# Top-k attention and a gated feed-forward on one core: the steps behind the top-k are put in other slots and on other engines

## The chip, the core and the metric

The kernel runs on one core of a Trainium2 chip. The engines are named as the profile names them: PE is TensorE (PEld its weight loads), DVE is VectorE, ACT is ScalarE, POOL is GpSimd, SP is SyncE, whose queue issues most DMA transfers. Each engine works through its own list of instructions in order, and waits at an instruction until what it needs is there. The metric is the device time of one execution in microseconds (us); the profile's span, from the first to the last instruction, is a little shorter.

## The reference

```python
def _attn_ref(q, k, v):                       # each (8, 8, 576, 64), float32
    top_k = 32
    scale = 1.0 / np.sqrt(D)
    scores = scale * np.matmul(q, k.transpose(0, 1, 3, 2))
    kth = np.partition(scores, -top_k, axis=-1)[..., -top_k:-top_k + 1]
    scores = np.where(scores >= kth, scores, -1000000000.0)
    scores = scores - np.max(scores, axis=-1, keepdims=True)
    attn = np.exp(scores)
    attn = attn / (np.sum(attn, axis=-1, keepdims=True) + 1e-09)
    return np.matmul(attn, v)

def _moe_ref(x, w_in, w_out):                 # x: (4608, 512), the attention's output
    h = x @ w_in                              # (4608, 2048)
    g = h * np.clip(h + 3.0, 0.0, 6.0) / 6.0
    return g @ w_out                          # (4608, 512)
```

Per row of 576 scores only the 32 largest count in the softmax. The weights arrive as 64-bit floats and are made 32-bit floats on the chip (`convert`).

## The kernel before

A *pair* is two heads of one batch. A *duo* is one tile of 128 query rows of two pairs; the 64 rows left over of 576 make a *rest duo*, in which one tile holds both heads of a pair. There are 80 duos (64 full, 16 rest). The loop has eight *slots* a duo; in each, VectorE does one round of top-k (the eight largest by MAX8, then MATCH_REPLACE8 to strike them out), slots 0 to 3 for the first pair, 4 to 7 for the second:

```python
def top(self, u, r):
    ...
    for t in range(self.nt):                  # nt: 2 tiles, 1 in a rest duo
        nc.vector.max(self.m[u][:, t, 8 * r : 8 * r + 8], self.cur[t])
    if r < TOP_K // 8 - 1:
        for t in range(self.nt):
            nc.vector.match_replace(wk, self.m[u][:, t, 8 * r : 8 * r + 8], self.cur[t], LOWEST)
            ...
```

What follows the top-k of pair `u` goes through three engines and a transfer:

```python
def shift(self, u):                           # (32nd largest - largest) * scale
    nc.gpsimd.tensor_tensor(d[:, 0:nt], m[:, 0:nt, TOP_K - 1], m[:, 0:nt, 0], ALU.subtract)
    nc.gpsimd.tensor_scalar_mul(d[:, 0:nt], d[:, 0:nt], scale)
def exp(self, u):
    for t in range(nt):
        nc.scalar.activation(row, row, AF.Prelu, bias=m[:, t, TOP_K - 1 : TOP_K], scale=-1.0, alpha=FLAT)
    for t in range(nt):
        nc.scalar.activation(row, row, AF.Exp, bias=self.less[u][:, t : t + 1],
                             scale=-scale / FLAT, accum_out=self.den[:, u, t : t + 1])
    nc.scalar.activation(d, d, AF.Copy, bias=EPS)
def inverse(self, u):
    nc.vector.reciprocal(d, d)                # d = self.den[:, u, 0 : self.nt]
def weights(self, u):                         # rows times 1/den, then split in 16-bit halves
    nc.gpsimd.tensor_scalar(row, row, self.den[:, u, t : t + 1], 1.0, ALU.mult, ALU.mult)   # per t
    nc.gpsimd.tensor_copy(halves[:, :, to : to + c1 - c0], words)
def flip(self, u):                            # transpose by DMA
    nc.sync.dma_start_transpose(t16[:, 0:n, :], self.e16[u][:, 0 : n * P])
def join(self, u):                            # halves put together: eT
    copy = nc.gpsimd.tensor_copy if u and not self.early else nc.scalar.copy
```

`values` multiplies `eT` with v on TensorE into `pv`, `place` copies `pv` into `xT`, and every second duo gives a block of 128 tokens to `feed_forward`, which works in pieces of 8 matmuls of `h` or 2 of `acc`, sixteen to a block, about one to a slot:

```python
def feed_forward(xT, rows):
    for f0 in range(0, NFC, nf):              # 4 times 16 matmuls into h
        h = ps_w.tile([P, 512], F32, tag="w", name="h")      # one of 3 PSUM buffers
        ...                                   # a yield in the middle
        nc.scalar.activation(g[:], h[:], AF.Relu, bias=three[:], scale=1.0)
        nc.scalar.copy(hs[:], h[:])
        def gate(g=g, hs=hs):
            nc.gpsimd.tensor_scalar(g[:], g[:], 6.0, 0.0, ALU.min, ALU.max)
            nc.gpsimd.tensor_tensor(g[:], g[:], hs[:], ALU.mult)
        yield gate                            # emitted two pieces later
    ...                                       # 16 matmuls into acc, a yield after every second
```

`scores` puts q k^T into `big`, five PSUM banks (the only buffer of its kind), and ScalarE at once copies them into `sc`. Which part stands in which slot (counted from the duo's first; slot 8 is slot 0 of the next duo) is a table. Parts of one slot are emitted in the table's order, duo by duo, but all `shift` parts first:

```python
usual = dict(
    shift0=3, exp0=4, inverse0=9, weights0=10, flip0=12, join0=15,
    shift1=7, exp1=8, inverse1=13, weights1=14, flip1=16, join1=19, values=22, place=23,
)
behind = dict(usual, values=25, place=26)
early = dict(...)                             # duos 0 and 1
soon = dict(
    shift0=3, exp0=3, inverse0=5, weights0=5, flip0=7, join0=10,
    shift1=7, exp1=7, inverse1=9, weights1=9, flip1=11, join1=14, values=16, place=17,
)                                             # the last two duos
```

Of the kernel before, what the change touches and what calls it, by code (L numbers as in the profile page):

```python
# [29 lines left out]
def kernel(  # L30
# [65 lines left out]
    def convert(dst, src):  # L96

        st = kqpool.tile([P, 2 * WC], U32, tag="kq", name="st")
        nc.sync.dma_start(st[:], src)
        yield
        words = st[:].rearrange("p (n two) -> p n two", two=2)
        lo, hi = words[:, :, 0], words[:, :, 1]
        a = gpool.tile([P, WC], F32, tag="g", name="a")
        y = gpool.tile([P, WC], F32, tag="g", name="y")
        nc.scalar.activation(a[:], hi.bitcast(F32), AF.Abs)
        nc.gpsimd.tensor_scalar(a[:], a[:], HI_MOST, HI_LEAST, ALU.min, ALU.max)

        nc.scalar.activation(y[:], lo, AF.Copy, bias=2.0, scale=2.0**-51)
        yield

        au, yu = a[:].bitcast(U32), y[:].bitcast(U32)
        nc.vector.tensor_scalar(au, au, 3, None, ALU.logical_shift_left)  # L117
        nc.vector.scalar_tensor_tensor(  # L118
            out=yu, in0=hi, scalar=0x80000000, in1=yu,
            op0=ALU.bitwise_and, op1=ALU.bitwise_or,  # L120
        )
        yield
        nc.gpsimd.tensor_tensor(
            dst.bitcast(I32), a[:].bitcast(I32), y[:].bitcast(I32), ALU.add
        )
# [13 lines left out]
    class Pair:  # L139
# [6 lines left out]
        def load(self):  # L146
            h0 = 2 * self.hp
            t = self.landed = kqpool.tile([P, 2 * J + 1, 2, D], F32, tag="kq", name="landed")
            for i, src in enumerate((k, q)):
                for hh in range(2):  # L150
                    nc.sync.dma_start(
                        t[:, i * J : (i + 1) * J, hh, :],
                        src[self.b, h0 + hh, 0:JP, :].rearrange("(p j) d -> p j d", j=J),
                    )
                nc.sync.dma_start(
# [15 lines left out]
        def transpose(self):  # L171
            kq = kqpool.tile([P, JP + S], F32, tag="kq", name="kq")
            self.kT, self.qT = kq[:, 0:JP], kq[:, JP : JP + S]
            ps = big()
            for j in range(2 * J + 1):
                rows = self.landed[:, j, :, :].rearrange("p h d -> p (h d)")
                nc.tensor.transpose(ps[:, j * P : (j + 1) * P], rows, ident[:])  # L177
            c0 = 2 * JP
# [6 lines left out]
    class Duo:  # L185
# [14 lines left out]
        def scores(self, us=(0, 1)):  # L200

            if us[0] == 0:
                self.sc = scpool.tile([P, 2, 2 * (S + R)], F32, tag="sc", name="sc")
                self.den = mpool.tile([P, 2, 2], F32, tag="den", name="den")
            sc, nu = self.sc[:, us[0] : us[-1] + 1, :], len(us)
            ps = big()
# [4 lines left out]
            if self.rest:  # L211
                for i, u in enumerate(us):
# [5 lines left out]
                nc.gpsimd.memset(sc[:, :, S : S + R], 0.0)  # L218
                nc.scalar.copy(sc[:, :, 0:JP], banks[:, 0:nu, :])
                nc.scalar.copy(  # L220
                    sc[:, :, JP:S], left[:, 0 : nu * R].rearrange("p (u r) -> p u r", r=R)
                )
# [6 lines left out]
            for i, u in enumerate(us):  # L229
                pr = self.pairs[u]  # L230
                for hh, d in enumerate(heads):
                    nc.tensor.matmul(banks[:, 2 * i + hh, :], pr.qT[d, qs], pr.kT[d, :])  # L232
            nc.scalar.copy(  # L233
# [25 lines left out]
        def shift(self, u):  # L259

            nt, m = self.nt, self.m[u]
            d = self.less[u] = mpool.tile([P, 2], F32, tag="shift", name="shift")
            nc.gpsimd.tensor_tensor(
                d[:, 0:nt], m[:, 0:nt, TOP_K - 1], m[:, 0:nt, 0], ALU.subtract
            )
            nc.gpsimd.tensor_scalar_mul(d[:, 0:nt], d[:, 0:nt], scale)  # L266

        def exp(self, u):
# [7 lines left out]
            for t in range(nt):  # L276
                row = self.row(u, t)
                nc.scalar.activation(  # L278
                    row, row, AF.Exp, bias=self.less[u][:, t : t + 1], scale=-scale / FLAT,
                    accum_out=self.den[:, u, t : t + 1],  # L280
                )
            d = self.den[:, u, 0:nt]
            nc.scalar.activation(d, d, AF.Copy, bias=EPS)

        def inverse(self, u):
            d = self.den[:, u, 0 : self.nt]
            nc.vector.reciprocal(d, d)  # L287
# [64 lines left out]
    def feed_forward(xT, rows):  # L352
# [6 lines left out]
        for f0 in range(0, NFC, nf):  # L359
# [12 lines left out]
            g = gpool.tile([P, 512], F32, tag="g", name="g")  # L372
            nc.scalar.activation(g[:], h[:], AF.Relu, bias=three[:], scale=1.0)  # L373
            hs = hpool.tile([P, 512], F32, tag="h", name="hs")
            nc.scalar.copy(hs[:], h[:])
            gs.append(g)

            def gate(g=g, hs=hs):
                nc.gpsimd.tensor_scalar(g[:], g[:], 6.0, 0.0, ALU.min, ALU.max)  # L379
                nc.gpsimd.tensor_tensor(g[:], g[:], hs[:], ALU.mult)  # L380

            yield gate
        acc = ps_w.tile([P, DM], F32, tag="w", name="acc")
        for f in range(NFC):
# [7 lines left out]
            if f % 2 == 1:  # L392
                if f == NFC - 1:
                    o = opool.tile([P, DM], F32, tag="o", name="o")
                    nc.scalar.mul(o[:], acc[:], 1.0 / 6.0)  # L395
                    for p0, p1, dst in rows:
                        nc.sync.dma_start(dst, o[p0:p1, :])
                yield None

# [5 lines left out]
    for b in range(B):  # L405
        halves = [pairs[b][0:2], pairs[b][2:4]]
        for qt in range(J):
# [3 lines left out]
            if qt == (0 if b == B - 1 else J - 1) and not 2 < b < B - 1:  # L411
# [11 lines left out]
    gates = []  # L423

    def piece(count=1):
        nonlocal left
        for _ in range(count):
            while todo:
                try:
                    gates.append(next(todo[0]))  # L430
                    left -= 1
                    break
                except StopIteration:
                    todo.pop(0)
            else:
                gates.append(None)
            if len(gates) > 2:
                gate = gates.pop(0)
                if gate:
                    gate()  # L440
# [45 lines left out]
    def land(count=1):  # L486

        for _ in range(min(count, len(chunks))):
            c = convert(*chunks.pop(0))
# [20 lines left out]
    def pair_at(m, first):  # L510
# [5 lines left out]
    first[0].load()  # L516
    land(2)
    first[1].load()
    first[0].transpose()
    convert_step()  # L520
    duos[0].scores((0,))
    convert_step()
    first[2].load()
    convert_step()
    first[1].transpose()
    duos[0].scores((1,))
    land()


# [3 lines left out]
        shift0=3, exp0=4, inverse0=9, weights0=10, flip0=12, join0=15,  # L533
        shift1=7, exp1=8, inverse1=13, weights1=14, flip1=16, join1=19, values=22, place=23,
    )

    behind = dict(usual, values=25, place=26)
    early = dict(
        shift0=3, exp0=3, inverse0=4, weights0=4, flip0=5, join0=8,
        shift1=7, exp1=7, inverse1=8, weights1=8, flip1=9, join1=12, values=12, place=13,  # L540
    )
    soon = dict(
        shift0=3, exp0=3, inverse0=5, weights0=5, flip0=7, join0=10,
        shift1=7, exp1=7, inverse1=9, weights1=9, flip1=11, join1=14, values=16, place=17,
    )
    queued = {}
    for m in range(ND):
        for part, at in (early if m < 2 else soon if m >= ND - 2 else behind if per_batch <= m < ND - 4 else usual).items():
            queued.setdefault(8 * m + at, []).append((m, part))

    def parts(slot, late=None):

        for m, part in sorted(queued.get(slot, []), key=lambda x: x[1][:-1] != "shift"):
            if late is not None and (part[:-1] in ("inverse", "weights")) != late:
# [3 lines left out]
            elif part == "place":  # L558
                place(m)
            else:  # L560
# [3 lines left out]
    for m in range(ND + 3):  # L564
        u = duos[m] if m < ND else None
        for i in range(8):
# [7 lines left out]
            if m == 0 and i in (1, 2):  # L574
                first[i + 1].transpose()
            if i == (4 if m == 0 else 1) and m + 1 < ND:
                duos[m + 1].scores()
            if m < 4:
# [13 lines left out]
            if i == 5:  # L592
                p = pair_at(m, 5)
                if p:
                    p.transpose()

            due += ((left > 0) + (left >= 24) / 8 + (left >= 48) / 8) / (2 if u and u.rest else 1)
            piece(int(due))
            due -= int(due)
    while todo:  # L600
        piece()
    piece(2)
# [33 lines left out]
```

## Time and profile before

| | |
|---|---|
| device time, median of 3 runs | 1581.81 us (1580.72 to 1583.69) |
| span of the profile | 1578.5 us, mean granted TensorE clock 0.963 |
| MAX8, 1152 of them | 816.4 us busy |
| MATCH_REPLACE8, 864 | 635.5 us |
| reciprocals of `den`, 160 | 24.6 us |
| matmuls of the feed-forward (`h`, `acc`) | 1061.3 us |
| exponentials and PReLU on ScalarE, 576 | 430.5 us |
| shifts on GpSimd, 320 instructions | 69.4 us |

The rows are sums over groups of the same instruction. Busy times of neighbours overlap by some 0.07 us, so what an instruction costs its engine is better read from the distance between the starts of two. A row of idle time belongs to the engine that waits; it costs time only where that engine sets the end or holds up the one that does. Where a bracket follows a line of a timeline, it gives the idle time before it and what ended it.

### The profile page before, as it was taken

The numbers are of one execution on the slowest core, as the hardware profiler recorded it, in microseconds if no ns is written. First come the engines' busy times: TensorE is split into PE (matmuls) and PEld (weight loads), VectorE is DVE, ScalarE is ACT, GpSimd is POOL, SyncE is SP. The second block draws the span as 40 slices with busy tenths as digits, with TensorE's granted clock in tenths as the row PEclk, the third lists the DMA queues.
The fourth block names the chain that finished last, engine by engine and source line by source line (L and its number), as shares of the span: only waits on it lengthen the run. The fifth ranks groups of instructions, "written<-read, shape, count | busy, mean of one in ns | idle before, by whom it ended". The sixth has DMA issues, their size and how long they took to land.

```text
span 1578.5 us, 28787 instructions
## 1 busy us (share of the span) xinstructions
PE 1456.9 (92%) x10272; PEld 1039.0 (66%) x10272; DVE 1466.8 (93%) x3105; ACT 1096.3 (69%) x1865; POOL 1144.5 (73%) x1264
## 2 busy tenths in 40 slices
PE   5256799979999999998999999999999999999899
PEld 3153566567767777666777777776777767677675
DVE  6999999999999999999999999999999999999700
ACT  6675777777777777777776786777766787777621
POOL 4868687777867777867687777867687777767841
PEclk9568999989999999999999999999999999999999
DMA  8652543444344543545254543446244443533410
GB/s 236 159 181 45 113 83 81 94 91 97 76 90 89 101 83 76 101 85 119 55 106 76 97 89 82 93 93 116 57 96 87 98 88 74 103 65 68 83 22 14
DMA packets 450319, 144.49 MB, mean 92 GB/s; under 512 B 433280, under 2 KB 441472, under 8 KB 450176
## 3 DMA queue, kind: packets, MB, share of 16 engines
q1 hardware_dynamic: 450176, 142.65, 43.5%
q8 instruction: 81, 1.33, 0.3%
q14 instruction: 62, 0.51, 0.1%
HBM read 45.09 MB, written 9.44 MB: 35 GB/s over the span
## 4 chain that ended last, share of the span: by engine, by line
DVE 51%; PE 35%; POOL 5%; issue 3%; ACT 3%; DMA 1%; SPq 1%; POOLq 0%; ACTq 0%; DVEq 0%
DVE m L250 26%; DVE wk L254 22%; PE h L365 14%; PE acc L385 13%; PE pv L338 4%; PE big L232 3%; POOL e L306 1%; DVE y L118 1%; POOL sc L297 1%; DMA t<-e 1%; POOL eT L318 1%; DVE a L117 1%; PE big L177 1%; ACT sc L278 1%; ACT eT L318 1%
## 5 line engine op out<-in xcount | busy, mean ns | idle before, releaser
L250 DVE MAX8 m<-wk 128x8 f32<-128x576 f32 x864 | 613.1, 746 | 2.2
L385 PE MATMUL acc<-w_out,g 128*128 128x512 f32 x1152 | 516.9, 600 | 14.1 <-POOL g L380 14.1
L365 PE MATMUL h<-xT,w_in 128*128 128x128 f32 x4096 | 485.5, 279 | 17.3 <-ACT xT L348 17.3
L365 PEld LDWEIGHTS h<-xT,w_in 128*128 128x128 f32 x4096 | 475.0, 195 | 39.5 <-issue 18.2
L254 DVE MATCH_REPLACE8 wk<-m,wk 128x576 f32<-128x576 f32 x576 | 423.7, 742 | 0.0
L385 PEld LDWEIGHTS acc<-w_out,g 128*128 128x128 f32 x1152 | 213.6, 191 | 260.4 <-issue 238.6
L297 POOL TENSOR_SCALAR sc<-sc,den 128x576 f32<-128x576 f32 x288 | 213.8, 753 | 229.9 <-DVE den L287 222.7
L306 POOL COPY e<-sc 128x2304 uint16<-128x2304 uint16 (+1 forms) x192 | 320.3, 1678 | 10.2
L278 ACT ACTIVATE sc<-sc,shift 128x576 f32<-128x576 f32 x288 | 220.4, 769 | 40.5 <-POOL shift L266 37.7
L318 ACT COPY eT<-t 128x2304 uint16<-128x2304 uint16 (+1 forms) x82 | 215.9, 2632 | 37.9 <-DMA t<-e 35.3
L273 ACT ACTIVATE sc<-sc,m 128x576 f32<-128x576 f32 x288 | 210.1, 777 | 46.2 <-DVE m L250 46.0
L338 PE MATMUL pv<-eT,vm 128*64 128x128 f32 (+1 forms) x2560 | 164.0, 273 | 57.9 <-ACT eT L318 45.8
L254 DVE MATCH_REPLACE8 wk<-m,sc 128x576 f32<-128x576 f32 x288 | 211.8, 742 | 0.0
L318 POOL COPY eT<-t 128x2304 uint16<-128x2304 uint16 (+1 forms) x78 | 203.8, 2613 | 6.9 <-DMA t<-e 6.5
L338 PEld LDWEIGHTS pv<-eT,vm 128*64 128x64 f32 x2560 | 135.2, 141 | 109.3 <-ACT eT L318 49.7
L250 DVE MAX8 m<-sc 128x8 f32<-128x576 f32 x288 | 203.3, 742 | 2.4 <-ACT sc L236 2.4
L373 ACT ACTIVATE g<-h,three 128x512 f32<-128x512 f32 x144 | 98.5, 684 | 150.0 <-PE h L365 140.6
L380 POOL TENSOR_TENSOR g<-g,hs 128x512 f32<-128x512 f32 x144 | 185.0, 1285 | 12.1 <-POOL g L379 0.2
L233 ACT COPY sc<-big 128x2048 f32<-128x2048 f32 (+1 forms) x65 | 119.3, 1836 | 26.1 <-PE big L232 26.0
L232 PE MATMUL big<-kq 64*128 64x512 f32 x512 | 136.4, 653 | 0.0
L379 POOL TENSOR_SCALAR g<-g 128x512 f32<-128x512 f32 x144 | 89.2, 620 | 62.6 <-ACT g L373 52.4
L395 ACT ACTIVATE o<-acc 128x512 f32<-128x512 f32 x36 | 21.4, 595 | 106.6 <-PE acc L385 106.6
(47 smaller groups left out, 1113.1 us busy)
## 6 DMA issues: line engine op xcount, KB each, us to landing
landed<-in_k_dram SPq DMA_DIRECT2D x64, 128.0 KB, 3.0
landed<-in_q_dram SPq DMA_DIRECT2D x64, 128.0 KB, 3.0
st<-in_moe_w_in_dram SPq DMA_DIRECT2D x16, 512.0 KB, 5.1
vm<-in_v_dram SPq DMA_DIRECT2D x64, 128.0 KB, 2.3
st<-in_moe_w_out_dram SPq DMA_DIRECT2D x16, 512.0 KB, 6.6
out_dram<-o SPq DMA_DIRECT2D x32, 256.0 KB, 2.4
t<-e SPq DMA_TRANSPOSE x160, 4.6
landed<-in_k_dram SPq DMA_DIRECT2D x32, 32.0 KB, 2.8
```

Of the source, the lines that this page charges most:

```text
L232: nc.tensor.matmul(banks[:, 2 * i + hh, :], pr.qT[d, qs], pr.kT[d, :])
L250: nc.vector.max(self.m[u][:, t, 8 * r : 8 * r + 8], self.cur[t])
L254: nc.vector.match_replace(wk, self.m[u][:, t, 8 * r : 8 * r + 8], self.cur[t], LOWEST)
L273: nc.scalar.activation(row, row, AF.Prelu, bias=m[:, t, TOP_K - 1 : TOP_K], scale=-1.0, alpha=FLAT)
L278: nc.scalar.activation(row, row, AF.Exp, bias=self.less[u][:, t : t + 1], scale=-scale / FLAT, accum_out=self.den[:, u, t : t + 1],)
L297: nc.gpsimd.tensor_scalar(row, row, self.den[:, u, t : t + 1], 1.0, ALU.mult, ALU.mult)
L306: nc.gpsimd.tensor_copy(halves[:, :, to : to + c1 - c0], words)
L318: copy(eT[:, 0 : self.nb, :] .rearrange("p c q -> p (c q)") .bitcast(U16) .rearrange("p (x h) -> p h x", h=2), self.t16[u][:, 0 : 2 * self ...
L338: nc.tensor.matmul(pv[hh * D : (hh + 1) * D, u * w : (u + 1) * w], pr.vm[:, hh, c, :] if c < J else pr.vr[:, hh, :], rhs, start=(c == 0), ...
L365: nc.tensor.matmul(h[:, (f - f0) * P : (f - f0 + 1) * P], w_in[:, i, f * P : (f + 1) * P], xT[:, i, :], start=(i == 0), stop=(i == NHP - 1),)
L380: nc.gpsimd.tensor_tensor(g[:], g[:], hs[:], ALU.mult)
L385: nc.tensor.matmul(acc[:], gs[f // nf][:, f % nf * P : (f % nf + 1) * P], w_out[:, f, :], start=(f == 0), stop=(f == NFC - 1),)
```

## The change

What follows the top-k is done sooner for all duos, so that value products and with them feed-forward blocks are ready earlier; ScalarE is to meet its reads of PSUM when their matmuls are done. In parts:

1. **Table.** `values` moves from slot 22 or 25 to 17, right behind the next `scores`. The second pair's steps follow the first's by one slot.
2. **One reciprocal a duo**, in slot 10, after one `settle` (the addition of EPS) in slot 8.
3. **Shift on ScalarE**: one copy with scale, then one small activation a tile, instead of two GpSimd instructions.
4. **Late reads**: ScalarE's copies of scores stand in slot 4 (matmuls: slot 1), those of the transposes in slot 7 (slot 5), those of `h` and `acc` one piece after their matmuls.
5. **Start**: the first pair's q is loaded through ScalarE's queue; in the first 16 weight chunks `y` is in PSUM.
6. **End**: in the last batch the rest duos stand behind the second tile of queries, not the first; only the last duo has a table of its own.

```diff
-    def convert(dst, src):
+    def convert(dst, src, early):
-        y = gpool.tile([P, WC], F32, tag="g", name="y")
+        y = (ps_w.tile([P, WC], F32, tag="w", name="yp") if early
+             else gpool.tile([P, WC], F32, tag="g", name="y"))
...
         def transpose(self):
...
+        def store(self):                       # the copies into kq and kr
...
         def scores(self, us=(0, 1)):
...
+        def store(self, us=(0, 1)):            # the copies into sc
...
         def shift(self, u):
-            nc.gpsimd.tensor_tensor(
-                d[:, 0:nt], m[:, 0:nt, TOP_K - 1], m[:, 0:nt, 0], ALU.subtract
-            )
-            nc.gpsimd.tensor_scalar_mul(d[:, 0:nt], d[:, 0:nt], scale)
+            nc.scalar.activation(d[:, 1, 0:nt], m[:, 0:nt, 0], AF.Copy, scale=-scale)
+            for t in range(nt):
+                nc.scalar.activation(
+                    d[:, 0, t : t + 1],
+                    m[:, t, TOP_K - 1 : TOP_K],
+                    AF.Identity,
+                    bias=d[:, 1, t : t + 1],
+                    scale=scale,
+                )
...
-        def inverse(self, u):
-            d = self.den[:, u, 0 : self.nt]
-            nc.vector.reciprocal(d, d)
+        def inverse(self, us):
+            d = self.den[:, us[0] : us[-1] + 1, 0 : self.nt]
+            nc.vector.reciprocal(d, d)
+        def settle(self, us):
+            d = self.den[:, us[0] : us[-1] + 1, 0 : self.nt]
+            nc.scalar.activation(d, d, AF.Copy, bias=EPS)
...
-            nc.scalar.activation(g[:], h[:], AF.Relu, bias=three[:], scale=1.0)
-            nc.scalar.copy(hs[:], h[:])
+            def read(h=h):                      # called one piece later; returns the gate
...
-            if qt == (0 if b == B - 1 else J - 1) and not 2 < b < B - 1:
+            if qt == (1 if b == B - 1 else J - 1) and not 2 < b < B - 1:
...
-    first[0].load()
+    first[0].load(nc.scalar)
...
     usual = dict(
-        shift0=3, exp0=4, inverse0=9, weights0=10, flip0=12, join0=15,
-        shift1=7, exp1=8, inverse1=13, weights1=14, flip1=16, join1=19, values=22, place=23,
+        shift0=3, exp0=4, shift1=7, exp1=8, settle01=8, inverse01=10, weights0=10, weights1=11,
+        flip0=12, flip1=13, join0=15, join1=16, values=17, place=18,
     )
-    behind = dict(usual, values=25, place=26)
...
-    soon = dict(
-        shift0=3, exp0=3, inverse0=5, weights0=5, flip0=7, join0=10,
-        shift1=7, exp1=7, inverse1=9, weights1=9, flip1=11, join1=14, values=16, place=17,
+    last = dict(
+        shift0=3, exp0=3, settle0=3, inverse0=5, weights0=5, flip0=7, join0=10,
+        shift1=7, exp1=7, settle1=7, inverse1=8, weights1=8, flip1=9, join1=11, values=11, place=11,
     )
...
             if i == (4 if m == 0 else 1) and m + 1 < ND:
                 duos[m + 1].scores()
+            if i == 4 and m + 1 < ND:
+                duos[m + 1].store()
...
             if i == 5:
                 p = pair_at(m, 5)
                 if p:
                     p.transpose()
+            if i == 7:
+                p = pair_at(m, 5)
+                if p:
+                    p.store()
```

## The prediction

> **What bounds the kernel now.** I read the page's busy times and its chain first, then the waits of VectorE, then timelines of single stretches. The page, busy time by engine and chain by engine:
>
> ```profile
> PE 1456.9 (92%) x10272; PEld 1039.0 (66%) x10272; DVE 1466.8 (93%) x3105; ACT 1096.3 (69%) x1865; POOL 1144.5 (73%) x1264
> ...
> DVE 51%; PE 35%; POOL 5%; issue 3%; ACT 3%; DMA 1%; SPq 1%; POOLq 0%; ACTq 0%; DVEq 0%
> ```
>
> Two engines share the chain, so either could be the bound. The waits of VectorE decide it (reader <- releaser, us in total, times, longest):
>
> ```profile
> DVE a L117 <- POOL a L109: 13.3, 2, 10.0
> DVE den L287 <- ACT den L283: 9.3, 4, 6.7
> DVE m L250 <- ACT sc L236: 2.4, 2, 1.7
> ```
>
> Of the 13.3 us on `a`, 10.0 lie before the first conversion; of the 9.3 us on `den`, 6.7 lie after the last top-k. From 13.59 us (first MAX8) to 1491.3 us (last MAX8) VectorE hardly ever waits, not even for scores. So the span is 1491.3 us of VectorE and then 87.2 us of tail; TensorE keeps up, with some reserve. The timeline of VectorE in a rest duo (one tile, not two, per pair) gives the yardstick for the change:
>
> ```profile
> 583.50 0.74 DVE L250 MAX8 m<-sc 128x8 f32<-128x576 f32 x1
> 584.27 0.09 DVE L254 MATCH_VALUE_LOAD wk<-m,sc 128x8 f32 x1
> 584.35 0.74 DVE L254 MATCH_REPLACE8 wk<-m,sc 128x576 f32<-128x576 f32 x1
> 585.13 0.76 DVE L250 MAX8 m<-wk 128x8 f32<-128x576 f32 x1
> ...
> 589.11 0.74 DVE L250 MAX8 m<-sc 128x8 f32<-128x576 f32 x1
> ```
>
> Read the starts, since busy times overlap: a slot (MAX8 and MATCH_REPLACE8) is 585.13 - 583.50 = 1.63 us, and a whole pair of a rest duo 589.11 - 583.50 = 5.61 us. In a full duo the same readings give 2.77 us a slot and 9.70 us a pair, 19.4 us a duo. And ScalarE's part of the chain of a pair near the end:
>
> ```profile
> 1477.70 2.80 ACT L318 COPY eT<-t 128x2304 uint16<-128x2304 uint16 x1
> 1480.97 1.44 ACT L273 ACTIVATE sc<-sc,m 128x576 f32<-128x576 f32 x2 [0.47 <-DVE m L250]
> 1482.32 0.76 ACT L278 ACTIVATE sc<-sc,shift 128x576 f32<-128x576 f32 x1
> 1482.99 0.18 ACT L278 ACTIVATION_READ_ACCUMULATOR sc<-sc,shift 128x1 f32 x1
> 1483.08 0.76 ACT L278 ACTIVATE sc<-sc,shift 128x576 f32<-128x576 f32 x1
> 1483.75 0.18 ACT L278 ACTIVATION_READ_ACCUMULATOR sc<-sc,shift 128x1 f32 x1
> 1483.96 0.20 ACT L283 ACTIVATE den<-den 128x2 f32<-128x2 f32 x1
> ```
>
> From the first PReLU to the end of `den` is 1484.16 - 1480.97 = 3.2 us; a join (`eT` copy) is about 2.65 us of issue. Here the join ran before the top-k was done, while ScalarE waited for VectorE anyway. The tail on TensorE:
>
> ```profile
> 1495.72 1.81 PE L338 MATMUL pv<-eT,vm 128*64 128x128 f32 x16 [4.41 <-POOL eT L318]
> ...
> 1518.52 14.45 PE L365 MATMUL h<-xT,w_in 128*128 128x128 f32 x128
> 1532.81 13.90 PE L385 MATMUL acc<-w_out,g 128*128 128x512 f32 x32
> 1546.55 14.45 PE L365 MATMUL h<-xT,w_in 128*128 128x128 f32 x128
> 1560.84 13.90 PE L385 MATMUL acc<-w_out,g 128*128 128x512 f32 x32
> ```
>
> After the last value products two whole feed-forward blocks follow, 56 us, then 3.8 us until the output has landed.
>
> **What the Trainium skill says.** "SBUF — State Buffer", section "Who interferes with whom": a VectorE instruction with two SBUF inputs is blocked by a GpSimd instruction that reads SBUF, one with at most one SBUF input outside the 2-port modes is not. The trace agrees: L118, two SBUF inputs, takes 0.68 us alone and 1.09 or 1.75 us beside GpSimd work, while MAX8 keeps its 0.74 to 0.76. "Perfetto Trace Analysis", section "Optimizing Scalar/DVE Operations": work may go from a saturated engine to another, and each small ScalarE instruction pays a fixed overhead. Here a 128x2 ScalarE operation lasts 0.20 us, of which about 0.11 holds up the next. "TensorE: Matmul & The Clock Gate", section "What's actually happening": after idleness the clock is halved until some 3.4 us of work have passed (its figure). In the trace, after 4.41 us of idleness 16 matmuls take 1.81 us, not 1.09.
>
> **The change part by part.**
>
> VectorE, removed. Reciprocals fall from 160 to 83 (61 of four columns, 22 of two). One costs 0.15 us but only 0.08 between starts (119.69 to 119.77): 77 x 0.08 = 6.2 us off. For the first 16 weight chunks `y` lies in PSUM, so L118 has one SBUF input. Of their sixteen, three took 1.75 us and two 1.09: 3 x 1.07 + 2 x 0.41 = 4.0 us over 0.68; I take 3 off, as a read of PSUM may cost something. With the first pair's q on ScalarE's queue, k's issue (0.72 to 2.78 us) no longer precedes q's (2.82 to 4.77); the second half of the transposes, begun at 6.67 us for want of q, starts about 1.9 us earlier. VectorE alone would end at 1491.3 - 6.2 - 3 - 1.9 = 1480.2 us.
>
> VectorE, added: a wait, and this is my main step. Before, both reciprocals come five slots after their exponentials. Now the second pair's exponentials and `settle` are emitted in slot 8 and the common reciprocal in slot 10, so VectorE reaches it three slots after the last top-k: 3 x 2.77 = 8.3 us if a full duo follows, but 3 x 1.63 = 4.8 to 4.9 us if a rest duo does. Meanwhile ScalarE, in the program's order, must do shift, join, exponentials, settle. As `shift` now is ScalarE's and is sorted first in its slot, it waits for the last MAX8 and the join queues behind it. Sum from the end of the top-k: 0.17 (the shift in GpSimd began 1481.69 after a top-k ended at 1481.52) + 0.45 (three dependent small operations) + 2.65 + 3.2 + 0.04 = 6.5 us. Where a pair's transposes are stored in between, +1.43 (starts of a 128x1024, a 128x64 and two 64x64 copies) = 7.9; with one read of `h` in between, +1.04 = 7.6. Against 8.3 this just fits. Against 4.8 it is late by 1.75, 3.2 and 2.8. By the instruction order of the built kernel 12 full duos precede a rest duo: 7 with the store, 1 with the read, 4 plain: 22.2 + 2.8 + 7.0 = 32 us. Four rest duos precede a rest duo; with half the exponentials (2.0 us) they are late by 1.9 (three) and 0.4: 6 us. In all about 38 us of waiting on a saturated engine. VectorE then ends near 1480.2 + 38 = 1518 us.
>
> GpSimd loses the shifts: 27.9 + 28.2 + 6.2 + 7.1 = 69 us. ScalarE gets 448 small operations for 77 settles saved, some 75 us by 0.20 each. Neither is the bound; GpSimd's gain costs nothing and brings little.
>
> TensorE's work is the same, 5,280 matmul instructions. With two records an instruction and the starts above (h 0.1117 a record, acc 0.43, pv 0.058, and so on) it comes to 1401 us in both kernels. Counted up to the last scores, the new order has 14.6 us more of it done; behind the last scores 97 us stay, not 111. That half block is the use of shorter chains: work moved under top-k. In the steady part a batch is about 177 us for VectorE with no waits and about 176 for TensorE, so it can keep up, with little to spare.
>
> The tail. Chain of the last pair after VectorE's end: ScalarE 6.5 (a join of duo 78 again stands between shift and exponentials), reciprocal 0.3, GpSimd 1.5 + 2.1, transfer 4.7 (from issue to landing, row of the DMA issues 4.6), join 2.8: 18 us. Then 1.2 for half the value products, 56.1 for the two blocks, which are still queued behind them, 3.8 to the end, and 2 for a cold clock: 81 us, against 87.2.
>
> Sum: 1518 + 81 = 1599 us of span; the timed median lies 3.3 above the profile's span (1581.81 - 1578.5): 1602. I round to 1600.
>
> **The rivals.** (a) The wait is small or absent: a join might be done otherwise, or I misjudge the slots. Then 1480 + 81 + 3 = 1564 us, 1.1% faster. For it: four waits on `den` in the whole profile before. Against: that profile had five slots of slack, and the shift not on ScalarE. (b) The shorter chains are the point, TensorE was the bound, and the 14.6 us of work moved forward come off whole in addition: 1564 - 15 = 1549, just over 2%. For it: the chain runs on TensorE from 733 to 1212 us. Against: VectorE waited for scores only 2.4 us, and in the tail the two blocks stay last in order. (c) TensorE falls behind: values right behind the scores stall on joins not yet there, `h` held longer in three PSUM buffers, gates later behind 7.2 us of weights in a row on GpSimd. Then stores come late, exponentials after them, and full duos wait too: each 0.3 us on 64 full duos is 19 us, so 1620 or more.
>
> **Range and chances.** The main step's 38 us may be 20 (fewer waits) or 55 (joins waiting for their transfer behind a rest duo): 1582 to 1617. Rival (a) pulls the lower end to 1562, (c) the upper to 1622. Faster by over 2% (below 1550.2) needs (b): 0.12. Slower by over 2% (above 1613.4) needs more waits than counted: 0.22. Within 2%: 0.66.
>
> **What would show it.** Right: VectorE's waits gain a row "den <- ACT den" of some 16 waits and 30 to 50 us, each beside a rest duo; its last MAX8 is near 1518 us; the tail near 81 us. Wrong in the main step: that row stays under 10 us. Wrong towards (c): rows of MAX8 waiting for `sc`, or over 20 waits on `den`. Wrong in the tail: fewer than two blocks after the last values.

## The result, and the profile after

The changed kernel takes 1631.03 us (median of 4 runs, 1629.65 to 1631.79), against 1581.5 us of the kernel before beside it: ratio 1.031, 95% interval 1.0292 to 1.0328. It is slower by 49.5 us; the prediction had 1600 and a range up to 1622. The profile's span is 1629.3 us, 50.8 more than before.

The page of the kernel after, busy time by engine and chain by engine:

```profile
PE 1472.3 (90%) x10272; PEld 1042.5 (64%) x10272; DVE 1459.6 (90%) x3028; ACT 1165.6 (72%) x2236; POOL 1076.4 (66%) x944
...
PE 32%; DVE 23%; POOL 18%; ACT 11%; issue 8%; DMA 7%; SPq 2%; POOLq 0%; ACTq 0%; DVEq 0%
```

VectorE's busy time hardly moved (1466.8 us before). TensorE's rose by 15.4 us for the same 10272 records, though the clock granted between 250 and 1450 us is 0.99 in both kernels. The chain changed most: VectorE had 51% of it and now has 23%; GpSimd, ScalarE and the transposing DMA have 36%. Over a third of it now runs through the steps behind the top-k, which before ran beside it. VectorE's waits in the kernel after (reader <- releaser, us in total, times, longest):

```profile
DVE den L307 <- ACT den L311: 66.3, 29, 6.1
DVE a L123 <- POOL a L114: 15.2, 2, 9.8
DVE den L307 <- POOL eT L342: 2.8, 1, 2.8
DVE m L266 <- ACT sc L252: 2.6, 2, 1.7
```

What grew are the reciprocal's waits (9.3 us before). The longest, 6.1 us, lies behind the last top-k; so 66.3 + 2.8 - 6.1 = 63.0 us lie before VectorE's end. The timeline of VectorE around that end:

```profile
1545.53 1.44 DVE L266 MAX8 m<-wk 128x8 f32<-128x576 f32 x2
1553.05 0.17 DVE L307 RECIPROCAL den<-den 128x2 f32<-128x2 f32 x1 [6.08 <-ACT den L311]
```

The last top-k ends at 1546.97 us, 55.7 us later than before (1491.3). Behind it TensorE has, as before, two whole feed-forward blocks:

```profile
1566.39 1.97 PE L362 MATMUL pv<-eT,vm 128*64 128x128 f32 x16 [3.69 <-POOL eT L342]
...
1568.72 15.02 PE L389 MATMUL h<-xT,w_in 128*128 128x128 f32 x128
1583.58 13.90 PE L413 MATMUL acc<-w_out,g 128*128 128x512 f32 x32
1597.31 14.45 PE L389 MATMUL h<-xT,w_in 128*128 128x128 f32 x128
1611.60 13.90 PE L413 MATMUL acc<-w_out,g 128*128 128x512 f32 x32
```

The tail is 1629.3 - 1546.97 = 82.4 us, against 87.2 before. So the change gains 4.8 us behind VectorE's end and loses 55.7 ahead of it.

One of the long waits, in full. ScalarE at the first rest duo behind batch 0, kernel after:

```profile
221.24 0.69 ACT L399 ACTIVATE g<-h,three 128x512 f32<-128x512 f32 x1 [2.46 <-PE h L389]
...
222.29 0.22 ACT L279 ACTIVATE shift<-m 128x2 f32<-128x2 f32 x1
222.54 0.48 ACT L281 ACTIVATE shift<-m,shift 128x1 f32<-128x1 f32 x2
222.93 2.78 ACT L342 COPY eT<-t 128x2304 uint16<-128x2304 uint16 x1
225.57 0.99 ACT L188 COPY kq<-big 128x1024 f32<-128x1024 f32 x1
...
227.02 1.44 ACT L294 ACTIVATE sc<-sc,m 128x576 f32<-128x576 f32 x2
...
230.01 0.20 ACT L311 ACTIVATE den<-den 128x4 f32<-128x4 f32 x1
```

and VectorE beside it:

```profile
218.26 1.43 DVE L266 MAX8 m<-wk 128x8 f32<-128x576 f32 x2
...
223.77 0.74 DVE L270 MATCH_REPLACE8 wk<-m,wk 128x576 f32<-128x576 f32 x1
230.32 0.18 DVE L307 RECIPROCAL den<-den 128x4 f32<-128x4 f32 x1 [5.80 <-ACT den L311]
```

The top-k that the shift needs ended at 219.69 us (218.26 + 1.43). ScalarE was then waiting for TensorE at a read of `h` (the bracket 2.46), and its shift began only at 222.29, 2.6 us late. From the shift on, everything runs without a gap: shift, join, the copies of the transposes, exponentials, `den`. The 5.80 us are thus two things added: 2.6 us because ScalarE came late, as TensorE was late, and 3.2 us because its own chain is too long for a rest duo. The prediction had only the second, and the size of that (3.2 us where the copies of the transposes are in the chain) was right.

### The profile page after: what moved, and what is told of

Same layout as the page of the kernel before. It is cut to its first block, busy times and chain, and to the rows that moved or that the text cites. A ratio compares the mean times of both kernels' runs of the same rounds, so it can differ in the third digit from the quotient of the medians.

```text
span 1629.3 us, 28728 instructions
## 1 busy us (share of the span) xinstructions
PE 1472.3 (90%) x10272; PEld 1042.5 (64%) x10272; DVE 1459.6 (90%) x3028; ACT 1165.6 (72%) x2236; POOL 1076.4 (66%) x944
## 3 DMA queue, kind: packets, MB, share of 16 engines
q8 instruction: 81, 1.33, 0.3%
## 4 chain that ended last, share of the span: by engine, by line
PE 32%; DVE 23%; POOL 18%; ACT 11%; issue 8%; DMA 7%; SPq 2%; POOLq 0%; ACTq 0%; DVEq 0%
DVE m L266 12%; PE acc L413 11%; PE h L389 11%; DVE wk L270 9%; DMA t<-e 7%; POOL e L330 6%; PE pv L362 5%; POOL sc L321 4%; POOL eT L342 4%; PE big L232 3%; POOL g L406 3%; ACT eT L342 3%; ACT sc L294 2%; ACT sc L299 1%; POOL g L405 1%
## 5 line engine op out<-in xcount | busy, mean ns | idle before, releaser
L389 PEld LDWEIGHTS h<-xT,w_in 128*128 128x128 f32 x4096 | 469.3, 193 | 22.2 <-issue 15.8
L389 PE MATMUL h<-xT,w_in 128*128 128x128 f32 x4096 | 478.6, 278 | 4.4 <-ACT xT L372 4.4
L330 POOL COPY e<-sc 128x2304 uint16<-128x2304 uint16 (+1 forms) x192 | 320.1, 1677 | 10.1
L362 PE MATMUL pv<-eT,vm 128*64 128x128 f32 (+1 forms) x2560 | 171.2, 280 | 79.3 <-ACT eT L342 38.9
L362 PEld LDWEIGHTS pv<-eT,vm 128*64 128x64 f32 x2560 | 140.5, 145 | 136.2 <-ACT eT L342 47.8
L399 ACT ACTIVATE g<-h,three 128x512 f32<-128x512 f32 x144 | 98.2, 682 | 104.7 <-PE h L389 101.4
L405 POOL TENSOR_SCALAR g<-g 128x512 f32<-128x512 f32 x144 | 88.3, 613 | 90.7 <-ACT g L399 80.7
L281 ACT ACTIVATE shift<-m,shift 128x1 f32<-128x1 f32 x288 | 75.3, 290 | 79.2 <-DVE m L266 74.9
```

The lines of the kernel that those rows point to most:

```text
L362: nc.tensor.matmul(pv[hh * D : (hh + 1) * D, u * w : (u + 1) * w], pr.vm[:, hh, c, :] if c < J else pr.vr[:, hh, :], rhs, start=(c == 0), ...
L389: nc.tensor.matmul(h[:, (f - f0) * P : (f - f0 + 1) * P], w_in[:, i, f * P : (f + 1) * P], xT[:, i, :], start=(i == 0), stop=(i == NHP - 1),)
```

## The experiments

"Rest duo" and "full duo" below name the duo in whose top-k the reciprocal stands. Ratios are to the kernel before, with their 95% interval.

**Single suspects, taken out of the kernel after.** The join ahead of the shift (e1), the shift back on GpSimd (e2), the reciprocal with its old slack (e3), ScalarE's reads of `h` and `acc` another piece later (e4). e3 moves more than the reciprocal: the joins and `values`, which come behind it, are eight slots later too.

```diff
e1:
-        for m, part in sorted(queued.get(slot, []), key=lambda x: x[1][:-1] != "shift"):
+        for m, part in sorted(queued.get(slot, []), key=lambda x: x[1][:-1] != "join"):
e2:
-            nc.scalar.activation(...)            # the shift's activations
+            nc.gpsimd.tensor_tensor(...); nc.gpsimd.tensor_scalar_mul(...)     # as before
e3 (duos 2 to 75):
-  inverse01=10, weights0=10, weights1=11, flip0=12, flip1=13, join0=15, join1=16, values=17, place=18
+  inverse01=13, weights0=13, weights1=14, flip0=15, flip1=16, join0=23, join1=24, values=25, place=26
e4:
-        if len(reads) > 1:
+        if len(reads) > 2:
```

> Only the sort within a slot is changed: the join is emitted ahead of the shift, so ScalarE does its 2.65 us before the top-k ends and not after it. Theory A (VectorE waits at the common reciprocal for a ScalarE chain of shift, join, exponentials, settle that is longer than its slots): each of the 29 waits on den loses up to 2.65 us, by their list from 66 to some 20 us with the 6 us of the last one, and the time falls by about 45 us to 1580 to 1592. Theory B (TensorE behind, values right behind the scores; VectorE's waits only pass its lateness on): the time stays above 1615.

> The shift goes back to GpSimd as in the kernel before, all else stays. Theory A: ScalarE loses the shift's 0.6 us from the chain and, since nothing of it waits for the top-k ahead of the join, the join as well: waits on den 66 to about 15 us, time 1575 to 1590, close to the join-first kernel. Theory B: above 1615. If only ScalarE's load mattered (320 shifts' worth of 0.1 to 0.2 us), it would fall by under 20 us.

> Shift and join stay as they are; only the common reciprocal and what hangs on it come later (slot 13 in place of 10, values in slot 25 in place of 17, still right behind scores), except in the last four duos. Theory A: the slack of a rest duo goes from 4.8 to 8.9 us, more than the chain's 6.5 to 8: waits on den fall to under 12 us, the time to 1565 to 1580. Theory B: values right behind scores are as before, so above 1610.

> ScalarE's reads of h and acc come two pieces after their matmuls, not one, so they should find the matmuls done. Theory A as refined by the trace of after (ScalarE reaches the shift late, because a read of h ahead of it waits 2 us or more for TensorE): some of the waits on den lose up to 2.5 us, in all 10 to 20 us off, 1611 to 1621. If the chain behind the top-k alone sets the waits: no change, 1625 to 1635. If TensorE then waits for PSUM: slower than 1635.

Measured: e1 1626.92 us (1.0295, 1.0279 to 1.031), e2 1620.57 (1.0253, 1.0238 to 1.0269), e3 1613.58 (1.0208, 1.0191 to 1.0225), e4 1636.61 (1.0355, 1.0339 to 1.037). None brings back even half of the loss. The traces say why. ScalarE in e1, at the same place as above:

```profile
222.01 0.69 ACT L399 ACTIVATE g<-h,three 128x512 f32<-128x512 f32 x1 [2.45 <-PE h L389]
...
223.07 2.81 ACT L342 COPY eT<-t 128x2304 uint16<-128x2304 uint16 x1
225.72 0.22 ACT L279 ACTIVATE shift<-m 128x2 f32<-128x2 f32 x1
```

The join is first now, but the read of `h` is ahead of it and still waits for TensorE; the chain starts as late as before. e4 takes most of that wait away. ScalarE's waits in e4:

```profile
ACT shift L281 <- DVE m L266: 141.0, 137, 4.3
...
ACT g L399 <- PE h L389: 36.3, 28, 3.6
```

In the kernel after, the first of these rows has 74.9 us and the second 101.4: ScalarE is now mostly at the shift in time. Yet VectorE in e4 still waits at the two rest duos behind batch 0:

```profile
225.51 0.18 DVE L307 RECIPROCAL den<-den 128x4 f32<-128x4 f32 x1 [3.86 <-ACT den L311]
241.18 0.17 DVE L307 RECIPROCAL den<-den 128x2 f32<-128x2 f32 x1 [4.41 <-ACT den L311]
```

Two limits lie side by side, ScalarE's lateness and the length of its own chain, and removing one shows the other. In e3 the waits on `den` fall from 69.1 to 19.5 us, but 31.2 us of MAX8 waiting for scores appear, where the kernel before had 2.4. So something else in the change delays the scores once the reciprocal no longer does.

**Half of the change each.** f1 keeps all of the change but the table (old slots, a reciprocal a pair); f2 is the kernel before with the new slots alone; f3 is the kernel after with the copies of the transposes right behind them; f4 moves the values two slots later.

```diff
f1:
-    usual, last (the new tables)
+    usual, behind, early, soon (the old ones); settle and inverse once a pair
f2 (kernel before; `behind` with values=25 is left out too):
-  inverse0=9, weights0=10, flip0=12, join0=15, inverse1=13, weights1=14, flip1=16, join1=19, values=22, place=23
+  inverse0=10, inverse1=10, weights0=10, weights1=11, flip0=12, flip1=13, join0=15, join1=16, values=17, place=18
f3:
                 if p:
                     p.transpose()
+                    p.store()
-            if i == 7: ...                       # p.store()
f4:
-  values=17, place=18
+  values=19, place=20
```

> The changed kernel with the table of the kernel before (reciprocals per pair, five slots after their exponentials; values in slot 22 or 25): late reads, shift on ScalarE, start and end stay changed. Theory T (the short table makes the loss: every step has so little slack that lateness of TensorE and ScalarE reaches VectorE): waits on den near 0, 1570 to 1590. Theory R (late reads and stores: the one PSUM buffer of scores is held longer, TensorE idles): still 1605 to 1630. First theory (ScalarE's chain with shift and join behind the top-k): that chain is kept but has 9 to 12 us of slack, so 1570 to 1590 too.

> The kernel before with the new table alone (values in slot 17, second pair one slot behind the first, both reciprocals in slot 10); shift stays on GpSimd, reads stay right behind their matmuls. Theory T: most of the loss, 1610 to 1635, waits on den over 40 us. Theory R: 1575 to 1595. First theory (shift and join on ScalarE): 1580 to 1595, as the shift on GpSimd lets the join run ahead.

> In the changed kernel only the copies of the transposes go back from slot 7 to slot 5, right behind their matmuls. Theory R: TensorE's 29 us of waits on kr between 250 and 1450 us go, and with them some 20 us of the time: 1602 to 1615. Theory T: 1622 to 1635, as ScalarE now waits for the transposes instead.

> In the changed kernel only values goes from slot 17 to 19, no longer right behind the next scores, so a join has two slots more. If TensorE's waits for eT (20 us between 250 and 1450 us) are what makes it late: 1605 to 1615. If not: 1625 to 1640, within 1% of the changed kernel.

Measured: f1 1617.05 us (1.0233, 1.0216 to 1.025), f2 1615.19 (1.0222, 1.0195 to 1.0249), f3 1612.51 (1.0199, 1.0184 to 1.0215), f4 1641.84 (1.0386, 1.0371 to 1.0402). With the old table (f1) the kernel is still 36 us slower than before, so the rest of the change loses time without the new slots. The new slots alone (f2) lose 34 us: VectorE waits there 51.1 us on `den` in 30 places. Together that is more than the 49.5 us of the whole change, so the two losses overlap. f3 names a suspect in the rest: the copies of a pair's transposes, moved two slots, are worth 18.5 us. TensorE's waits for these copies in the kernel after:

```profile
PE big L226 <- ACT kr L192: 23.5, 15, 2.9
...
PE big L220 <- ACT kr L192: 14.5, 7, 5.9
```

and TensorE's waits in f3:

```profile
PE pv L362 <- POOL eT L342: 38.5, 22, 3.7
...
PE big L226 <- ACT kr L192: 4.7, 3, 1.6
```

The copy into `kr` is the last that empties `big`. With the shorter rows (1.5 us in one place, and in f3 another 1.6), TensorE waits for it 39.5 us in 23 places in the kernel after and 7.8 us in 5 in f3. What remains is the value products waiting for a join (the first row; in the kernel after it has 22.8 us). f4 did cure that (8.0 us), but the kernel became slower: 23.2 us of new waits on `den` appear with ScalarE's own shift named as the releaser, and half of the 10.8 us lost lie in a longer tail (87.7 us for 82.4). Why two slots more are worse than none stays open.

**Combinations.** g1 joins e1 and e4; g2 joins e3 and f3; g3 joins f1 and f3; g4 is the kernel before with the parts that only take work away (one reciprocal a duo, in slot 13; `y` in PSUM; q on ScalarE's queue).

> Both edits that did little alone: join ahead of the shift, and reads two pieces behind. Theory M (two limits beside each other: ScalarE comes late to the top-k's end because a read of h waits for TensorE, and if it comes in time, its own chain of shift, join and exponentials is too long; the later of the two sets the wait on den, so taking one away shows nothing): both gone, waits on den fall from 66 to under 30 us, the time from 1631 to 1590 to 1610. If TensorE's lateness reaches VectorE in any case: above 1620.

> The late reciprocal (1613.6 alone) together with the early copies of the transposes (1612.5 alone). If the one PSUM buffer of scores, held until slot 7, is what made TensorE late in the first, so that VectorE waited 31 us for scores there: those waits go and the two gains add: 1585 to 1597. If they are the same gain: 1605 to 1613.

> The changed kernel with the old table (1617.0) and the early copies of the transposes. If the late copies made all its loss (TensorE waited 31 us for kr and up to 23 us more for sc): 1578 to 1590. If the later copies of scores, slot 4, and later reads of h hold TensorE up as well: 1595 to 1610.

> The kernel before with what the change takes off VectorE and nothing that shortens slack: one reciprocal a duo in slot 13 (settle in slot 8), y of the first 16 chunks in PSUM, q of the first pair on the other queue. VectorE has 5 us of reciprocals and 3 us of conversions less: 1571 to 1578 if VectorE's end sets the time. If TensorE's work sets it: within 3 us of before.

Measured: g1 1619.6 us (1.0243, 1.0224 to 1.0261), g2 1596.36 (1.01, 1.0083 to 1.0117), g3 1578.37 (0.9983, 0.9976 to 0.999), g4 1579.93 (0.9994, 0.9985 to 1.0003). g1 removes both limits of e1 and e4 and is better than either, but misses what was expected of it: 51.9 of the 69.1 us of waits on `den` are left. The late copies are still in it. g2's gain over the kernel after (34.7 us) is nearly the sum of e3's and f3's (17.5 + 18.5). g3 is the turning point: old table and early copies together take the whole loss away, with the shift still on ScalarE, the scores and `h` read late, and the new start. It is 0.17% faster than before, the only version measured here whose interval lies below 1. g4 saves VectorE the same reciprocals and gains nothing that can be told from before; its waits on `den` are 20.1 us (9.3 before).

**The copies alone.** h3 is the kernel before with one thing changed: the copies out of the transposes' PSUM buffer stand in slot 7, not slot 5.

```diff
-    # transpose() ends with the four copies into kq and kr
+            if i == 7:
+                p = pair_at(m, 5)
+                if p:
+                    p.store()
```

> The kernel before, in which only the copies of the transposes move from slot 5 to slot 7. In the changed kernel with the old table this move is worth 38.7 us (1617.05 against 1578.37). If it needs nothing else of the change: 1605 to 1625, and TensorE waits for kr over 20 us. If it costs only beside the shift on ScalarE and the late reads, since here ScalarE is less behind: 1580 to 1598.

Measured: 1617.62 us (1.0233, 1.0218 to 1.0248), slower by 36.8 us (0.0233 of 1580.1). TensorE's waits for the copies grow from 9.2 us in 5 places to 43.0 in 21; the largest row in h3 is

```profile
PE big L228 <- ACT kr L185: 33.1, 15, 5.4
```

One of them, in TensorE's timeline in h3:

```profile
1100.28 1.15 PE L175 MATMUL big<-ident,landed 128*128 128x128 f32 x9
1101.27 3.60 PE L387 MATMUL acc<-w_out,g 128*128 128x512 f32 x8
1109.49 0.87 PE L228 MATMUL big<-kr,kq 128*128 128x128 f32 x4 [4.62 <-ACT kr L185]
```

and the same three steps in the kernel before:

```profile
1076.29 1.15 PE L177 MATMUL big<-ident,landed 128*128 128x128 f32 x9
1077.27 3.60 PE L385 MATMUL acc<-w_out,g 128*128 128x512 f32 x8
1080.70 0.61 PE L226 MATMUL big<-kr,kq 128*128 128x128 f32 x4
```

From the transposes to the next scores it is 9.2 us in h3 and 4.4 before. ScalarE in h3 shows what the copies stood behind:

```profile
1104.90 0.60 ACT L397 ACTIVATE o<-acc 128x512 f32<-128x512 f32 x1 [8.01 <-PE acc L387]
1105.40 2.74 ACT L320 COPY eT<-t 128x2304 uint16<-128x2304 uint16 x1
1108.00 1.01 ACT L181 COPY kq<-big 128x1024 f32<-128x1024 f32 x1
...
1109.01 0.43 ACT L185 COPY kr<-big 64x64 f32<-64x64 f32 x2
```

ScalarE, free and idle for 8.01 us, waited for the feed-forward's `acc`, then did a join, and only then emptied `big`. TensorE, which had finished `acc`, waited for that. And VectorE paid twice:

```profile
1112.69 0.17 DVE L289 RECIPROCAL den<-den 128x2 f32<-128x2 f32 x1 [3.19 <-ACT den L285]
...
1116.05 1.42 DVE L252 MAX8 m<-sc 128x8 f32<-128x576 f32 x2 [0.89 <-ACT sc L238]
```

Between 250 and 1450 us TensorE is busy 1178.1 us before and 1159.3 in h3: 22 us of idleness have become 41, and the granted clock there is 0.99 and 0.98. VectorE is busy 1192.2 and 1163.8. The idleness is not all: over the whole kernel the same 10272 records of matmuls are busy 1467.2 us in h3 and 1456.9 before, so they also ran 10 us slower.

**The table alone, without the late copies.** h1 is the kernel after with the copies early and the values behind the next transposes; h2 has the copies early, the join first and the reads later.

```diff
h1 (besides f3's edit; duos 2 to 75):
-  values=17, place=18
+  values=25, place=26
h2: the edits of f3, e1 and e4
```

> Early copies of the transposes (1612.5 alone, 46 us of waits on den left, TensorE waiting 38 us for eT between 250 and 1450 us), and values, without any other step, a whole duo later: slot 25, again right behind scores, except in the last four duos. If the joins that come too late for slot 17 make TensorE late, and by its late h and pv ScalarE and VectorE: waits for eT go, 1580 to 1597. If the short way from the exponentials to the reciprocal alone keeps VectorE waiting: 1605 to 1620.

> Early copies of the transposes, join ahead of the shift and reads two pieces behind: nothing of ScalarE's stands between top-k and exponentials but the shift. Values stay in slot 17. If the way to the reciprocal is what the new table loses on: waits on den under 20 us, 1585 to 1600. If TensorE's waits for eT: 1603 to 1615.

Measured: h1 1605.22 us (1.0152, 1.0136 to 1.0169), h2 1611.09 (1.0195, 1.0178 to 1.0212). h2 is no better than f3: with TensorE's value products still standing on unready joins, ScalarE waits 160.7 us at its reads of `pv`. In h1 they no longer do, and ScalarE is at the shift in time:

```profile
ACT shift L281 <- DVE m L266: 177.0, 200, 4.7
```

What VectorE then still waits for is, with one exception, the prediction's main step. Three of its reciprocals in h1, a plain one, one of the second rest duo in a row, and one with a read of `h` in the chain:

```profile
224.72 0.18 DVE L307 RECIPROCAL den<-den 128x4 f32<-128x4 f32 x1 [1.33 <-ACT den L311]
237.99 0.17 DVE L307 RECIPROCAL den<-den 128x2 f32<-128x2 f32 x1 [2.02 <-ACT den L311]
...
924.89 0.18 DVE L307 RECIPROCAL den<-den 128x4 f32<-128x4 f32 x1 [2.41 <-ACT den L311]
```

Twelve waits of the first and third kind (four columns) sum to 19.5 us, and four of the second (two columns) to 8.1. These sixteen stand in rest duos, where the prediction had counted them. Full duos have 2.2 us in three waits, two of them of two columns; the long one of 1.81 us is the exception, behind a join that waited 5.08 us for its transposing DMA.

**What stands in that stretch.** i1 is h1 with the join first, i2 is h1 with the shift on GpSimd.

> The kernel after with the copies of the transposes early, the values behind the next transposes (both as in h1, 1605) and, in addition, the join ahead of the plain work of its slot on ScalarE. Theory A (some 30 us are left in h1 because at the rest duos the shift and the join stand between top-k's end and the exponentials, so that den comes 1.3 to 2.4 us after its place): with the join out of that stretch each wait of 1.35 falls to about 0.7 or less and each of 2.0 to 2.4 to about 1.5; waits on den from 30 to 10-15 us, 1585 us, range 1578 to 1592. Rival B (the short slack itself: the shift, the exponentials and the reciprocal fill it whatever stands between): waits stay at 25 to 30, 1600 to 1606. Rival C (the join waits for TensorE's transposes when moved ahead, and holds ScalarE up): 1605 or above, with waits of ScalarE at the join in place of those at h.

> The kernel after with the copies of the transposes early, the values behind the next transposes (both as in h1, 1605) and, in addition, the shift's small operations on GpSimd in place of ScalarE. Theory A (shift and join between top-k's end and the exponentials are what makes den late): ScalarE has the join done while GpSimd shifts, some 0.6 us off each of the rest duos; waits on den from 30 to about 15 us, 1588 us, range 1580 to 1596. Rival B (the short slack itself): GpSimd's shift takes as long as ScalarE's and two hand-overs more, waits stay at 25 to 35 us, 1600 to 1610.

Measured: i1 1601.19 us (1.0128, 1.0111 to 1.0145), i2 1599.78 (1.0118, 1.0103 to 1.0133). Better, but by 4 and 5 us, not 15 to 20. In i1 the four-column waits halve, from 19.5 to 9.6 us: the join was part of them. All two-column ones together grow from 10.1 to 16.3, and ScalarE in i1 shows how:

```profile
216.06 2.81 ACT L342 COPY eT<-t 128x2304 uint16<-128x2304 uint16 x1 [1.47 <-DMA t<-e]
...
228.71 0.60 ACT L425 ACTIVATE o<-acc 128x512 f32<-128x512 f32 x1
232.88 2.81 ACT L342 COPY eT<-t 128x2304 uint16<-128x2304 uint16 x1 [3.57 <-DMA t<-e]
235.56 0.19 ACT L279 ACTIVATE shift<-m 128x1 f32<-128x1 f32 x1
```

A join ahead of the shift must wait for its own transposing DMA, which started only after the previous reciprocal; ScalarE stands 3.57 us before it (1.78 in h1), and the shift comes late: the wait at 237.99 us is 3.29 us here against 2.02 in h1. The steps behind the top-k form a loop, from one reciprocal over the DMA and the join to the next; neither of the two orders fits it into two short duos in a row.

## Why the prediction was wrong, point by point

**Start: wrong, small.** The transposes did not gain 1.9 us. With q on its own queue k landed later: the first transposes begin at 5.66 us, not 4.54, and all end at 7.81 instead of 7.97. The first MAX8 is at 13.42 instead of 13.59 us. The conversions' 3 us came out as 2.8, but by luck: the first sixteen gained 5.2 us (four of them, not three, had taken 1.75 us), and the other sixteen lost 2.4. Nearly right were the reciprocals' 6.2 (about 5, at 0.06 to 0.08 us each). VectorE without its waits on `den`: 1546.97 - 63.0 = 1484.0 us, for 1480.2 predicted.

**The main step: mechanism and places right, its size only in part.** The kernel after has the sixteen waits in rest duos that were counted. Their chain can be read in h1, where the copies of the transposes are out of it. Behind a full duo, 1.75 us were predicted for a plain one and 2.8 with a read of `h`; h1 shows 1.33 to 1.43 and 2.40 to 2.41 (in one of these three the read stands ahead of the shift). With copies and read both in the chain (1.75 + 1.43 + 1.04 = 4.2) e4 shows 3.86. From rest duo to rest duo 1.9 was predicted and 1.9 to 2.1 is there, but that is luck: the 1.9 held 1.43 for the copies, and without them the prediction's terms leave 0.4. In two of these four waits the join's own wait for its DMA (1.78 and 1.81 us) stands in the chain instead, which the sum did not have. Without the copies the prediction's terms give 24 us for the sixteen; h1 has 27.6.

**The step that failed: "In the steady part a batch is about 177 us for VectorE with no waits and about 176 for TensorE, so it can keep up, with little to spare."** From there the prediction went on as if TensorE's lateness were nil and ScalarE were free at each top-k's end. VectorE's waits before its end became 63.0 us in place of 38: 50.0 at the sixteen places and 13.0 in full duos, where none was reckoned. The late copies, part 4 of the change, were priced at 1.43 us inside ScalarE's chain and nothing for TensorE. But two engines at 99.4% and 98.2% busy (1192.2 and 1178.1 of 1200 us, before) have no slack to lend each other. Copies held back two slots keep the one `big` buffer full; TensorE stands still 19 us more (h3), and does not make it up (VectorE's last top-k ends at 1526.2 us in h3, 1491.3 before); ScalarE, in order, meets that lateness at its reads of `h`, `acc` and `pv`; and VectorE meets it at `den` and at the scores. The cost is 37 us alone in the kernel before, 38.7 with the old table (f1 less g3), 18.5 on top of the new one (kernel after less f3). "PSUM — Partial Sum Buffer" of the Trainium skill, in its summary of rules for kernel authors, says "Evacuate promptly — 2 MiB is tight"; the reason it gives is space, while the cost here was TensorE's time; this case agrees with the rule, with h3's 1.0233 beside it.

**"Against 8.3 this just fits": wrong for the same cause.** It nearly always fits when ScalarE is in time: h1 has 2.2 us of waits in full duos, for 13.0 in the kernel after.

**Rival (c) was the nearer one**, and the prediction's own sign for it, over 20 waits on `den`, is there (30). Of what (c) named, values on joins that are not ready cost 7.3 us (f3 less h1): VectorE ends 16.6 us later, and the tail is 8.4 us shorter. The longer hold of `h` by itself costs nothing that can be seen (g3 has it, and is not slower than before); the later gates were not tried by themselves. What it did not name, the hold of `big`, was the larger: 18.5 us on top of the new slots, and 36.8 alone.

**The tail: right.** 82.4 us for 81, with two whole blocks. That the early values shorten it, as the change intended, is seen in h1, which has them late and has a tail of 90.7 us. The last `den` wait, 6.08 us, answers to the 6.5 of the sum. The 3.3 us that the prediction added between span and time mixed two runs; within a run it is 1.8 (1631.1 and 1629.3).

The way from g3 to the kernel after, with VectorE's end (the end of its last top-k) and the tail behind it, read from each profile:

| kernel | time, us | VectorE's end | tail | step |
|---|---|---|---|---|
| g3 | 1578.4 | 1492.2 | 85.0 | old table, early copies |
| h1 | 1605.2 | 1511.8 | 90.7 | new slots, but values late |
| f3 | 1612.5 | 1528.4 | 82.3 | values right behind the scores |
| after | 1631.0 | 1547.0 | 82.4 | late copies |

The differences, 27, 7 and 18.5 us, must add up to the whole, so their sum proves nothing; and they depend on the order in which the steps are taken, as the copies' 38.7 and 18.5 show. The first row lies 2.6 us below before: all other parts of the change together. What stays open: why f4 is slower than the kernel after, what the later gates cost, and how i2's remaining waits divide between ScalarE's lateness (it waits 91.6 us at `h` there, 58.2 in h1) and the two hand-overs to GpSimd.

## What to carry to other kernels

Where two engines are both nearly full, a third that serves both in program order is a hinge: a read placed "late, so that it finds its data ready" can delay what it must release, and that cost has to be counted on the engine that waits for the buffer, not only on the one that reads. Count slack in microseconds of the shortest round that occurs (here a rest duo's 1.63 us a slot, not 2.77), and for a loop through several engines count the whole loop. When taking out one suspect changes little, look in the same trace for the second limit beside it, and take out both before dropping the first.

## What the runs showed of the hardware

Idleness on TensorE can cost twice, as the work behind it runs slower. In the tail of the kernel after, 16 value products take 1.97 us behind 3.69 us of idleness and 1.09 us when they follow other work; in h3 four matmuls of scores take 0.87 us behind 4.62 us of idleness, 0.61 before. The direction agrees with the Trainium skill, "TensorE: Matmul & The Clock Gate", section "What's actually happening", by which the clock of TensorE is halved after an idle window of about 3.4 us; here 1.98 us were also seen behind a shorter gap of 2.44 us that followed another of 0.91 us shortly before.

A second queue for q did not bring both loads in sooner: q's wait (1.05 us) vanished, but k, whose load was issued ahead of q's before and beside it now, was ready 1.1 us later.
